# A decode attention kernel on one core: the TensorE program as a four-turn loop of 664 instructions, with one V buffer and column-tiled output projections

## The chip, the cores and the metric

The kernel runs on one core of one Trainium2 chip. The metric is the device time of one execution in microseconds (us). The profile shows one execution of it; its span runs from the first to the last instruction of the program and is shorter than the time (by 1.4 to 1.8 us in nearly all runs here; one exception matters below).

Engines: PE is the matrix engine (TensorE), DVE the vector engine, ACT the scalar engine, POOL GpSimd, SP the engine whose queue issues the loads. Sixteen DMA engines carry the loads (the profile counts 16, and each large load has sixteen landings in the trace).

## The reference, cut to what matters

One decode step: layer norm, a sliding window attention over a cache (window 2048, 16 query heads on 8 KV heads of 256), an output projection, and a gate from a small FFN.

```python
xn = _layernorm(x)                                   # x: (2, 1, 448)
q = xn @ wq                                          # wq: 448 x 4096
k, v = last W = 2048 rows of k_cache, v_cache        # (2, 8, 8192, 256) each
o = softmax(q k^T * 256**-0.5) v
s = o @ wo                                           # wo: 4096 x 448
g = silu(relu(xn @ w1) @ w2)                         # w1: 448 x 1792, w2: 1792 x 448
return x + s * g
```

All is bf16. Nearly all work is loading: 16.8 MB of K, 16.8 MB of V, 10.5 MB of weights. The term s * g is small beside x. So agreement with the reference says little about the attention.

## The kernel before

The attention is cut into four units (one batch element and four KV heads each), with two K and two V buffers. A recording layer collects every engine's operations and emits them in a straight line, with semaphore waits between engines.

```python
def load_k(u):
    d_k[u] = pr.dma(SP, kbuf[u % 2][:, :], kv_src(u, A_k_cache), [st.get(("T", u - 2))])

def load_v(u, cuts=(0, NT)):
    deps = [None if u == 0 else st["q_mm"] if u == 1 else st["PV", u - 2]]
    ...
        d_v[u].append((hi, pr.dma(SP, vbuf[u % 2][:, lo * DH:hi * DH], ..., deps)))
```

T is the transpose of K on DVE, S the scores, Pt the turning of the probabilities, PV the product with V (all PE). The loads stand on the SP queue in the order wq (first part), k0, wq (rest), k1, v0, w1, w2, k2, v1, k3, v2, v3 (two parts), wo. wo comes in seven parts of 9, 7, 5, 4, 3, 2 and 2 row blocks j, and PE works through them at the end:

```python
WO_PARTS = [9, 7, 5, 4, 3, 2, 2]
...
for j in range(2 * NWO):                     # 32 row blocks of wo
    if j == 4:
        attend_spread(3)
    deps = deps + [d_wo.get(j), st["at_z", j // NWO]]
    for i in range(4):                       # four matmuls of 112 columns into one bank of 8 rows
        lo = j * D + i * NCOL
        m_o = pr.op(PE, mm(obk[0:NROW, 0:NCOL], at_z[:, ...], wo_sb[:, lo:lo + NCOL],
                           j == 0 and i == 0, j == 2 * NWO - 1 and i == 3), deps)
# [cut] tmp = obk * g, out = tmp + x, store
```

`idle_work(n)` runs n matmuls whose result nobody reads; they are there to keep PE's clock up.

Of the kernel before, what the change touches and what calls it, by code (L numbers as in the profile page):

```python
# [14 lines left out]
class _Op:  # L15
    __slots__ = ("eng", "fn", "deps", "dma", "needed", "value", "sem")

    def __init__(self, eng, fn, deps, dma):
        self.eng, self.fn, self.deps, self.dma = eng, fn, deps, dma
        self.needed, self.value, self.sem = dma, 0, None  # L20


class _Prog:


    def __init__(self, nc, es):
        self.nc, self.es = nc, es
        self.lists = {PE: [], DVE: [], ACTE: [], SP: [], POOL: []}

    def op(self, eng, fn, deps=()):  # L30
        o = _Op(eng, fn, [d for d in deps if d is not None], False)
        self.lists[eng].append(o)
        return o
# [6 lines left out]
    def run(self):  # L40
        n = 0
        for ops in self.lists.values():
            for o in ops:
                for d in o.deps:
                    d.needed = True
        for e, ops in self.lists.items():
            sem, count = self.es.enter_context(self.nc.semaphore(f"s_{e}")), 0
            for o in ops:
                if o.dma:
                    n += 1  # L50
                    o.sem, o.value = self.es.enter_context(self.nc.semaphore(f"d_{n}")), 16
                elif o.needed:
                    count += 1
                    o.sem, o.value = sem, count

        def emit(eng, ops):
            seen = {}
            for o in ops:
# [4 lines left out]
                for key, (sem, value) in want.items():  # L63
                    if value > seen.get(key, 0):
                        eng.wait_ge(sem, value)
                        seen[key] = value
                made = o.fn(eng) if o.fn else None
                if o.needed:
                    made.then_inc(o.sem, 16 if o.dma else 1)

        for name, e in (("gpsimd", POOL), ("sync", SP), ("scalar", ACTE), ("vector", DVE), ("tensor", PE)):
            emit(getattr(self.nc, name), self.lists[e])


def bass_recurrent_scan__sliding_block_cached__dense_activation_relu__decode_kernel(
# [21 lines left out]
    NU = 4  # L97
# [6 lines left out]
    WO_PARTS = [9, 7, 5, 4, 3, 2, 2]  # L104
    NWO = 16
# [5 lines left out]
    with es:  # L111
# [32 lines left out]
        qz = named("qz", [128, 16 * 64], BF)  # L144
# [15 lines left out]
        q_t = et[:, :].bitcast(F32).tensor  # L160
        ssum = named("ssum", [128, 1], F32)
        rs = named("rs", [128, NU], F32)
        pt = [named(f"pt{i}", [128, 512], BF) for i in range(2)]
# [37 lines left out]
        def load_k(u):  # L201
            d_k[u] = pr.dma(SP, kbuf[u % 2][:, :], kv_src(u, A_k_cache), [st.get(("T", u - 2))])

        def load_v(u, cuts=(0, NT)):
            deps = [None if u == 0 else st["q_mm"] if u == 1 else st["PV", u - 2]]
            d_v[u] = []
            for lo, hi in zip(cuts, cuts[1:]):
                d_v[u].append((hi, pr.dma(SP, vbuf[u % 2][:, lo * DH:hi * DH],
# [14 lines left out]
        p_z = [pr.op(POOL, lambda e, t=t: e.memset(t[:, :], 0.0)) for t in (qrep, spread, h_z, at_z)][-1]  # L223

        a_z = [pr.op(ACTE, lambda e, t=t: e.memzero(t[:, :])) for t in (obk, sbk, hbk, obk_last)][-1]
# [40 lines left out]

        def mm(out_ap, lhsT, rhs, start, stop=False, **kw):
# [15 lines left out]
        def do_T(u, blk):  # L283
            src = kbuf[u % 2][:, :].bitcast(F32).tensor
            dst = kt[blk][:, :].bitcast(F32).tensor
            st["T", u] = st["kt", u, blk] = pr.op(DVE, lambda e: e.transpose(  # L286
# [3 lines left out]
        def do_S(u, blk):  # L290
            b, v = divmod(u, 2)
            deps = [st["q"], st["kt", u, blk], st.get(("exp", u - 1)), a_z]
            for par in range(2):
                for i in range(4):
                    lo = 64 * (4 * i + 2 * v + b) + 8 * (2 * blk + par)
                    o = pr.op(PE, mm(sbk[32 * i:32 * i + 8, :], qz[:, lo:lo + 8], view(kt[blk], 2 * i + par, [[64, NT], [8, 8]]),
                                     blk == 0 and par == 0, blk == NBLK - 1 and par == 1, tile_position=(0, 32 * i)), deps)
                    deps = []
            st["S", u, blk] = o

        def softmax(u, fill=()):
            fill = list(fill)

            def meanwhile():
                if fill:
                    fill.pop(0)()

            meanwhile()
# [6 lines left out]
            meanwhile()  # L315
            a = st["exp", u] = pr.op(ACTE, lambda e: e.activation(  # L316
                e_sb, sbk[:, :], ACT.Exp, bias=bias[:, 0:1], accum_out=ssum[:, 0:1]),
                [v, st.get(("e_t", u - 1)), st.get(("gs", u - 1))])
            v = st["e_t", u] = pr.op(DVE, lambda e: e.transpose(e_t, e_sb), [a, st.get(("Pt", u - 1))])  # L319
            deps = [v, v_sp, st.get(("pt", u - 1))]  # L320
            for x in range(4):
                for g in range(4):
                    lo = 128 * (4 * x + g)
                    o = pr.op(PE, mm(view(pbk, 2 * x, [[8, 16], [1, 2]]), spread[:, lo:lo + 128],
                                     view(et, 512 + 2 * g, [[32, 16], [1, 2]]), g == 0, g == 3), deps)
                    deps = []
            st["Pt", u] = o
            v = st["pt", u] = pr.op(DVE, lambda e: e.tensor_tensor(  # L328
                out=view(pt[u % 2], 0, [[8, NT], [2, 4], [1, 2]]), in0=view(pbk, 0, [[2, NT], [0, 4], [1, 2]]),
                in1=view(hmask, 0, [[0, NT], [1, 4], [0, 2]]), op=ALU.mult), [o, v_hm, st.get(("PV", u - 2))])  # L330
            meanwhile()
            m = st["gs", u] = pr.op(PE, mm(mbk_ap(130, 1), gsum[:, :], ssum[:, 0:1], True, True), [v_gs, a, st["mbk"]])
            st["rs", u] = st["mbk"] = pr.op(DVE, lambda e: e.reciprocal(rs[:, u:u + 1], mbk_ap(130, 1)), [m])
            assert not fill
# [4 lines left out]
        def do_PV(u, gs=range(4)):  # L339
            bank, src, p = out_bank(u), vbuf[u % 2], pt[u % 2]  # L340
            for g in gs:
                deps = [next(d for hi, d in d_v[u] if hi >= 16 * g + 16), st["pt", u], a_z, st["obk"] if u < NU - 1 else None]
                for a in range(2):
                    for i in range(4):
                        t = 16 * g + 4 * i + 2 * a
                        o = pr.op(PE, mm(bank[32 * i:32 * i + 16, :],
                                         p[:, 8 * t:8 * t + 16], src[:, t * DH:(t + 2) * DH],
                                         g == 0 and a == 0, g == 3 and a == 1, tile_position=(0, 32 * i)), deps)
                        deps = []
            st["PV", u] = o  # L350

        def attend_scale(u):
            v = st["osb", u] = pr.op(DVE, lambda e: e.tensor_scalar(  # L353
                out=o_sb[:, :], in0=view(out_bank(u), 0, [[1, 512]]), scalar1=rs[:, u:u + 1], scalar2=None, op0=ALU.mult),
                [st["PV", u], st["rs", u], st.get(("oT", u - 1))])
            if u < NU - 1:
                st["obk"] = v

        def attend_turn(u):
            deps = [st["osb", u], v_fold, st["mbk"]]  # L360
# [6 lines left out]
            st["at", u] = st["mbk"] = pr.op(DVE, lambda e: e.tensor_tensor(  # L367
# [4 lines left out]
        def attend_spread(u):  # L372
            b, v = divmod(u, 2)
            o = st["m_at", u] = pr.op(PE, mm(mbk_ap(256, NWO), at_exp[:, :], fold16[:, :], True, True),
                                      [st["at", u], v_fold16, st["mbk"]])
            st["at_z", v] = st["mbk"] = pr.op(DVE, lambda e: e.tensor_copy(
                view(at_z, NWO * GAP * v + 3 + 4 * b, [[GAP, NWO]]), mbk_ap(256, NWO)), [o, p_z])

        def do_q():
# [8 lines left out]
            v = st["obk"] = pr.op(DVE, lambda e: e.tensor_scalar(  # L388
                out=q_n[:, :], in0=obk[:, :], scalar1=SCALE, scalar2=None, op0=ALU.mult), [o])
            m = pr.op(PE, mm(pbk[:, :], qrep[:, :], q_n[:, :], True, True), [v, v_qr])  # L390
            v = pr.op(DVE, lambda e: e.transpose(view(q_t, 0, [[1, 512]]), view(pbk, 0, [[64, 8], [1, 2], [2, 32]])), [m])
            for r in range(2):
                st["q"] = pr.op(DVE, lambda e, r=r: e.tensor_tensor(
                    out=view(qz, r, [[64, 16], [8, 8], [2, 4]]), in0=view(q_t, 256 * r, [[1, 16], [32, 8], [0, 4]]),
                    in1=view(gmask, 0, [[0, 16], [0, 8], [1, 4]]), op=ALU.mult), [v, v_gm])

        def do_H():
            deps = [st["w1"], v_xr, a_z]
# [11 lines left out]

        def do_F():
            deps = [st["w2"], st["h"]]
            for f in range(14):
                for i in range(4):
                    lo = W2_AT + f * D + i * NCOL
                    o = pr.op(PE, mm(view(fbk, 0, [[1, NCOL]], n=NROW), h_z[:, f * GAP + 3 - i:f * GAP + 3 - i + NROW],
                                     w2_sb[:, lo:lo + NCOL], f == 0 and i == 0, f == 13 and i == 3), deps)
                    deps = []
            st["F"] = o
            f_ap = view(fbk, 0, [[1, NCOL]], n=NROW)  # L420
            a_e = pr.op(ACTE, lambda e: e.activation(ea[:, :], f_ap, ACT.Exp, scale=-1.0), [o])
            st["a_e"] = a_e

        def gate():
            f_ap = view(fbk, 0, [[1, NCOL]], n=NROW)
            v_d = pr.op(DVE, lambda e: e.tensor_scalar(
                out=ea[:, :], in0=ea[:, :], scalar1=1.0, scalar2=None, op0=ALU.add), [st["a_e"]])
            v_rc = pr.op(DVE, lambda e: e.reciprocal(tmp[:, :], ea[:, :]), [v_d])
            st["g"] = pr.op(DVE, lambda e: e.tensor_tensor(
                out=g_sb[:, :], in0=f_ap, in1=tmp[:, :], op=ALU.mult), [v_rc])  # L430

        def idle_work(n):
            deps = [st["q"], p_id]
            for _ in range(n):
                pr.op(PE, mm(wbk[:, :], ident[:, :], q_n[:, :], True, True), deps)
                deps = []

        def scores(u):
            for blk in range(NBLK):
                do_T(u, blk)  # L440
                if u == 1 and blk == 3:
                    do_H()
                if blk == 1 and u > 1:
                    attend_turn(u - 2)
                if blk == 2 and u > 1:
                    attend_spread(u - 2)
                do_S(u, blk)

# [89 lines left out]
```

## Time and profile before

| | before |
|---|---|
| time, median | 111.43 us (111.37 to 111.62, 4 runs) |
| span of the profiled run | 109.8 us |
| loads | 44.11 MB |
| PE program (compiled instructions) | 1234 |
| last landing of a load | 107.33 us |
| last wo matmul ends | 107.93 us |

From the page of the kernel before: the span, the engines' busy time, and the DMA queues with packets, megabytes and the share of all sixteen engines' span that they took.

```profile
span 109.8 us, 1386 instructions
PE 61.3 (56%) x610; PEld 21.9 (20%) x612; DVE 61.7 (56%) x87; ACT 9.6 (9%) x18; POOL 3.1 (3%) x10
...
q1 hardware_dynamic: 3008, 44.11, 94.9%
q8 instruction: 4, 0.07, 0.2%
q10 hardware_dynamic: 36, 0.01, 0.0%
q14 instruction: 1, 0.01, 0.0%
```

No compute engine is busy for much over half of the span. Queue 8 carries four packets of instructions.

The table of stretches of the kernel before; the last three columns are PE's granted clock, the DMA engines' mean busy share and GB/s.

```profile
core 0: us, PE busy (x) PEld busy (x) DVE busy (x) ACT busy (x) POOL busy (x), PEclk, DMA share, GB/s
...
45.00:61.00 16.00, 11.66 (x158) 5.57 (x150) 10.02 (x14) 0.92 (x3) 0.00 (x0) 0.93 1.02 433
61.00:78.00 17.00, 11.00 (x87) 2.28 (x87) 12.53 (x17) 0.78 (x2) 0.00 (x0) 0.70 1.00 432
78.00:100.00 22.00, 16.34 (x138) 4.33 (x140) 13.46 (x17) 0.78 (x2) 0.00 (x0) 0.79 0.99 422
100.00:107.00 7.00, 6.52 (x121) 5.86 (x121) 1.08 (x3) 0.00 (x0) 0.00 (x0) 1.00 0.84 328
```

From 15 to 100 us the DMA share is 0.99 to 1.02. The loads bound the kernel.

The end of the chain that ended last, kernel before (start, length, what):

```profile
76.42 24.57 DMA kbuf<-in_A_wo_dram
...
101.02 0.95 PE obk L268 x16
...
102.09 5.86 PE obk L268 x112
...
107.97 0.27 DVE tmp L502
...
108.27 0.26 DVE out_sb L504
```

This view puts the last 7 us down to PE, because PE is busy with wo nearly without a pause. The records of the single instructions say more: PE's last eight matmuls start at 107.38, less than 0.05 us after the last load has landed at 107.33, after a short wait. PE and the loads arrive together here.

Each large load counts sixteen landings in the semaphore records, read here as one for each of the sixteen DMA engines. From the semaphore records of the trace, the landings of the last wo part, kernel before:

```
eleven engines  105.56 to 106.09
one engine      106.51
four engines    107.12  107.22  107.31  107.33
```

And the instruction packets of queues 8 and 14 in the same trace:

```
q8   46.18 us, 1102 ns, 16384 bytes
q14  57.25 us,  333 ns,  8192 bytes
q8   57.34 us, 1099 ns, 16384 bytes
q8   85.36 us, 1087 ns, 16384 bytes
q8  102.43 us, 1038 ns, 16384 bytes
```

Four packets of 16 KiB, four engines late by about 1.2 us; one packet of 8 KiB, one engine late by 0.5 us. In the same records one of sixteen landings is late after the first packet (w2: 49.83, the others by 48.53), two after the second (K: 59.47 and 59.55, besides the 58.75 of the 8 KiB packet; the others by 58.24), three after the third (95.78 to 96.01, besides 95.15; the others by 94.68). The records do not number the engines; that each packet hit another one is read from these counts.

### The profile page before, as it was taken

To read this page: it belongs to the slowest core of one execution; us is meant where nothing else is said; L and a number is where in the kernel's file an instruction comes from. 1 tells how busy PE (TensorE), PEld (TensorE's weight loads), DVE (VectorE), ACT (ScalarE), POOL (GpSimd) and SP (SyncE) were. 2 spreads that over 40 slices of the span, in tenths; PEclk is the share of its full clock that TensorE was granted. 3 is DMA by queue.
4 is the path that set the end of the run, shared out by engine and by line. 5 is a ranking of instruction groups with operands and counts; after the bars stand their busy time and mean duration, and the time that the engine had idled before them with its cause. 6 is when DMAs were issued, how large, how long until landed. Compare 5 with 4: busy or idle time off the path is not lost.

```text
span 109.8 us, 1386 instructions
## 1 busy us (share of the span) xinstructions
PE 61.3 (56%) x610; PEld 21.9 (20%) x612; DVE 61.7 (56%) x87; ACT 9.6 (9%) x18; POOL 3.1 (3%) x10
## 2 busy tenths in 40 slices
PE   0000000192699035999970498834039885997993
PEld 0000000020110030034930010112001011533992
DVE  1258039987200679986165999257499926504001
ACT  4990000000000200000200000020000002000000
POOL 7400000000000000000000000000000000000000
PEclk9999999999999965699998555799555699999999
DMA  4989989999899889998999999999999999899950
GB/s 69 505 382 418 501 379 403 448 513 394 382 454 501 382 374 416 415 532 382 418 474 430 394 406 513 406 394 418 501 406 394 445 430 430 361 414 412 393 208 1
DMA packets 3049, 44.19 MB, mean 402 GB/s; under 512 B 354, under 2 KB 612, under 8 KB 1508
## 3 DMA queue, kind: packets, MB, share of 16 engines
q1 hardware_dynamic: 3008, 44.11, 94.9%
q8 instruction: 4, 0.07, 0.2%
q10 hardware_dynamic: 36, 0.01, 0.0%
q14 instruction: 1, 0.01, 0.0%
HBM read 44.11 MB, written 0.00 MB: 402 GB/s over the span
## 4 chain that ended last, share of the span: by engine, by line
DMA 67%; DVE 18%; PE 11%; ACT 1%; issue 1%; SPq 0%
DMA kbuf<-in_A_k_cache_dram 45%; DMA kbuf<-in_A_wo_dram 22%; DVE kt L286 14%; PE obk L268 7%; PE sbk L268 4%; ACT et L316 1%; DVE et L319 1%; DVE rm L309 1%; PE pbk L268 1%; PE mbk L268 1%; DVE o_sb L353 1%; SPq L36 0%; DVE at_exp L367 0%; DVE tmp L502 0%; DVE out_sb L504 0%
## 5 line engine op out<-in xcount | busy, mean ns | idle before, releaser
L268 PE MATMUL sbk<-kt,qz 128*8 128x512 bf16 x128 | 31.1, 1072 | 17.4 <-DVE kt L286 15.2
L286 DVE STREAM_TRANSPOSE kt<-kbuf 128x2048 f32<-128x2048 f32 x16 | 35.9, 2286 | 7.4 <-DMA kbuf<-in_A_k_cache_dram 7.4
L268 PE MATMUL obk<-vbuf,xr 128*4 128x512 bf16 x28 | 3.2, 625 | 13.2 <-DMA vbuf<-in_A_wq_dram 13.2
L309 DVE TENSOR_REDUCE rm<-sbk 128x1 f32<-128x512 f32 x4 | 2.8, 692 | 12.3 <-PE sbk L268 12.3
L316 ACT ACTIVATE et<-sbk,bias 128x512 bf16<-128x512 f32 x4 | 2.7, 682 | 65.1 <-DVE bias L313 65.1
L268 PEld LDWEIGHTS sbk<-kt,qz 128*8 128x8 bf16 x128 | 2.2, 87 | 30.7 <-DVE kt L286 23.1
L268 PE MATMUL obk<-kbuf,at_z 128*8 128x112 bf16 x128 | 6.9, 213 | 0.2 <-DMA kbuf<-in_A_wo_dram 0.2
L268 PE MATMUL obk<-vbuf,pt 128*16 128x512 bf16 x96 | 6.4, 381 | 0.0
L268 PEld LDWEIGHTS obk<-kbuf,at_z 128*8 128x8 bf16 x128 | 6.3, 87 | 0.5 <-DMA kbuf<-in_A_wo_dram 0.2
L268 PE MATMUL pbk<-et,spread 128*128 128x32 bf16 x64 | 2.6, 193 | 6.3 <-DVE et L319 6.3
L319 DVE STREAM_TRANSPOSE et<-et 128x512 bf16<-128x512 bf16 x4 | 2.8, 711 | 4.9 <-ACT et L316 4.9
L268 PE MATMUL mbk<-ident,xg 2*128 2x2 bf16 x7 | 0.3, 164 | 8.0 <-DVE xg L235 8.0
L328 DVE TENSOR_TENSOR pt<-pbk,hmask 128x512 bf16<-128x512 f32 x4 | 2.8, 692 | 3.0 <-PE pbk L268 3.0
L268 PEld LDWEIGHTS pbk<-et,spread 128*128 128x128 bf16 x64 | 2.2, 99 | 9.7 <-DVE et L319 9.7
L268 PE MATMUL wbk<-q_n,ident 128*128 128x512 bf16 x14 | 3.7, 379 | 0.3 <-issue 0.3
L268 PEld LDWEIGHTS obk<-vbuf,xr 128*4 128x4 bf16 x28 | 0.8, 114 | 14.7 <-issue 14.7
L502 DVE TENSOR_TENSOR tmp<-obk,g_sb 8x112 f32<-8x112 f32 x1 | 0.3, 261 | 5.6 <-PE obk L268 5.6
L268 PEld LDWEIGHTS obk<-vbuf,pt 128*16 128x16 bf16 x96 | 2.5, 91 | 4.4 <-issue 1.6
L268 PEld LDWEIGHTS fbk<-wf,h_z 128*8 128x8 bf16 x56 | 2.8, 88 | 1.6 <-issue 1.6
L268 PE MATMUL fbk<-wf,h_z 128*8 128x112 bf16 x56 | 2.9, 213 | 0.0
L367 DVE TENSOR_TENSOR at_exp<-mbk,qmask 128x128 bf16<-128x128 f32 x4 | 1.2, 292 | 3.0 <-PE mbk L268 2.9
L268 PE MATMUL obk_last<-vbuf,pt 128*16 128x512 bf16 x32 | 2.3, 380 | 0.0
(69 smaller groups left out, 39.4 us busy)
## 6 DMA issues: line engine op xcount, KB each, us to landing
kbuf<-in_A_k_cache_dram SPq DMA_DIRECT2D x4, 4096.0 KB, 29.4
vbuf<-in_A_v_cache_dram SPq DMA_DIRECT2D x3, 4096.0 KB, 37.8
wf<-in_B_w_dram SPq DMA_DIRECT2D x2, 1568.0 KB, 43.1
vbuf<-in_A_v_cache_dram SPq DMA_DIRECT2D x1, 3072.0 KB, 20.8
vbuf<-in_A_wq_dram SPq DMA_DIRECT2D x1, 2560.0 KB, 19.7
vbuf<-in_A_wq_dram SPq DMA_DIRECT2D x1, 1024.0 KB, 5.0
vbuf<-in_A_v_cache_dram SPq DMA_DIRECT2D x1, 1024.0 KB, 22.7
kbuf<-in_A_wo_dram SPq DMA_DIRECT2D x1, 1008.0 KB, 24.6
```

The lines of the kernel that those rows point to most:

```text
L268: return lambda e: e.matmul(out_ap, lhsT=lhsT, rhs=rhs, start=start, stop=stop, skip_group_check=True, **kw)
L286: st["T", u] = st["kt", u, blk] = pr.op(DVE, lambda e: e.transpose(view(dst, 0, [[1, 32 * NT]]), view(src, 32 * blk, [[DH // 2, NT], [1, 3 ...
L309: v = pr.op(DVE, lambda e: e.tensor_reduce(out=rm[:, :], in_=sbk[:, :], axis=AX.X, op=ALU.max), [st["S", u, NBLK - 1]])
L316: a = st["exp", u] = pr.op(ACTE, lambda e: e.activation(e_sb, sbk[:, :], ACT.Exp, bias=bias[:, 0:1], accum_out=ssum[:, 0:1]), [v, st.get(( ...
L319: v = st["e_t", u] = pr.op(DVE, lambda e: e.transpose(e_t, e_sb), [a, st.get(("Pt", u - 1))])
L328: v = st["pt", u] = pr.op(DVE, lambda e: e.tensor_tensor(out=view(pt[u % 2], 0, [[8, NT], [2, 4], [1, 2]]), in0=view(pbk, 0, [[2, NT], [0, ...
L353: v = st["osb", u] = pr.op(DVE, lambda e: e.tensor_scalar(out=o_sb[:, :], in0=view(out_bank(u), 0, [[1, 512]]), scalar1=rs[:, u:u + 1], sc ...
L367: st["at", u] = st["mbk"] = pr.op(DVE, lambda e: e.tensor_tensor(out=view(at_exp, 0, [[16, 8], [8, 2], [1, 8]]), in0=view(mbk, 136, [[1, 8 ...
L502: v_t = pr.op(DVE, lambda e: e.tensor_tensor(out=tmp[:, :], in0=obk[0:NROW, 0:NCOL], in1=g_sb[:, :], op=ALU.mult), [m_o, st["g"]])
```

## The change

The intent: PE's straight program of 1234 instructions becomes a loop of four turns, one for each unit, so that the instruction packets seen beside the loads, four in the trace of the kernel before, no longer come in mid-run. For the loop's instructions to be the same in every turn, units 0 to 2 share one V buffer, the probability tile becomes one, and waits become tokens that are taken back after use. wo and w2 use four column tiles of the array side by side, with fewer instructions; the four partial sums are then folded with a small f32 matmul. The core of the diff:

```diff
+        nc.br("pe_all", engines=[t.engine])
+        with nc.body("pe_all", valid_engines=[t.engine]):
+            top = nc.cur_bb
+            nc.br("pe_visit", engines=[t.engine])       # the visit: jump ahead, and come back
+            nc.switch_bb("pe_back", parent=top)
+            ahead = t.mark_branch_hint_location()       # hint of the last branch, armed here
+            emit(t, pe[:at], seen)
+            with t.Fori(0, turns) as i:
+                # [cut] the parts of a turn, some under t.If(i == n) or t.If(i > n)
+            nc.br("pe_past", engines=[t.engine])
+            nc.switch_bb("pe_visit", parent=top)
+            t.nop()
+            nc.br("pe_back", engines=[t.engine])
+            nc.switch_bb("pe_past", parent=top)
+            emit(t, pe[at + len(loop):], seen)
+            t.reg_add(again, again, 1)
+            t.br_lt(again, 1, on_true="pe_all", on_false="pe_end").branch_hint(ahead)   # never taken
# [cut]
-            deps = [None if u == 0 else st["q_mm"] if u == 1 else st["PV", u - 2]]
+            deps = [None if u == 0 else st["q_mm"] if u == NU - 1 else st["PV", u - 1]]
-                d_v[u].append((hi, pr.dma(SP, vbuf[u % 2][:, lo * DH:hi * DH],
+                d_v[u].append((hi, pr.dma(SP, vbuf[u // (NU - 1)][:, lo * DH:hi * DH],
# [cut]
+        def tiled(bank, z, k, w, lo, first, last, deps):     # column tile k % 4, 448 columns at once
+            g = k % 4
+            return pr.op(PE, mm(view(bank, 0, [[1, D]], n=2, p0=32 * g), view(z, k * GAP + 3, [[4, 2]]), w[:, lo:lo + D],
+                                k < first, k >= last, tile_position=(0, 32 * g)), deps)
+        def fold_tiles(bank_ap, start, stop, deps):          # sel and sums are f32
+            for i in range(4):
+                o = pr.op(PE, mm(bank_ap, sel[:, 3 - i:3 - i + NROW], sums[:, i * NCOL:i * NCOL + NCOL], ...), deps)
# [cut] wo: row blocks 0 to 20 (TILED) tiled, 21 to 31 as before
+        m_t = do_wo(NWO, TILED)
+        idle_work(2)
+        v_w = pr.op(DVE, lambda e: e.tensor_copy(sums[:, :], view(obk, 0, [[1, D]])), [m_t, m_f])
+        do_wo(TILED, TILED + 4)                              # the fourth part
+        fold_tiles(view(hbk, 0, [[1, NCOL]], n=NROW), False, False, [v_w])
+        m_o = do_wo(TILED + 4, 2 * NWO)                      # the last three parts
```

## The prediction

> **What bounds it now.** The loads. The page gives 44.11 MB read over a span of 109.8 us; the table of stretches shows the 16 DMA engines 99 to 102% busy from 15 to 100 us; DMA has 67% of the chain of waits, while PE and DVE are 56% busy. In the trace's packet list each 32 KiB packet takes 1213 ns throughout, so [...]a late one stays late.
>
> Late ones exist. Queue 8 carries four 16,384-byte instruction packets, at 46.2, 57.3, 85.4 and 102.4 us, 1.1 us each: PE's program, about 1,220 instructions and waits. [...]After the first, one of w2's sixteen landings is 1.3 us after the rest. After all four, the last wo part has eleven landings at 105.6–106.1 us, one at 106.5 (an 8 KiB instruction packet of another queue) and four at 107.1–107.3: each fetch hit another engine. PE waits for 107.33, runs its last eight wo matmuls to 107.95; two DVE operations (0.5 us) and the store end it at 109.8.
>
> **What the change does.**
> 1. [...]mid-run fetches should go. [...]Worth at most 1.2 us: the last landing moves to 106.1–106.5. If the visit's fetch collides with the first wq load (from 1.7 us), one engine starts up to 1.2 us late and most is lost.
> 2. wo gets 21 column-tiled steps, four side by side (estimate from PV's 32 matmuls in 2.3 us: 0.06 us a step against 0.21 for four 112-column matmuls), 11 old ones, two f32 folds. PE's wo work (6.9 us) loses about 3 us, but PE already waited for landings, so directly this gains nothing; it lets PE follow earlier landings. The fold (0.7 us DVE copy; four f32 matmuls, estimated 0.4–0.75 us from the f32 ones of the trace) stands before the last three parts: after the part ahead of it lands, PE needs 0.85 + fold + 1.4 = 2.65–3.0 us, against 2.5 for the DMA limit. PE becomes the limit by 0.2–0.5 us.
> 3. One V buffer: v1 now waits for PV0 (about 53 us; k2 keeps DMA busy to 58), v2 for PV1 (about 72; k3 lasts to 77). Slack 3–5 us: no gap expected.
> 4. Branches, tokens and turn_q per unit (2 x 0.36 us DVE, from 0.725 us for the larger product at most halved): under the loads.
>
> Sum: last landing −1.0, PE tail +0.3: 110.7 us. Some weight lies on a colliding visit (no gain), less on refetches at the back edge. Range 109.9 to 112.2. Faster by over 2% 0.03, within 2% 0.88, slower by over 2% 0.09.
>
> **What would show it.** Step 1: queue 8 is empty after 5 us, and the last wo part's sixteen landings lie within 0.6 us, near 106.1; more packets, or one engine 1 us late from the first load on, refute it. Step 2: PE no longer waits for the last landing and ends at 106.9–107.4. Step 3: DMA over 97% busy from 15 to 100 us; a dip near 58 or 77 refutes it. Step 4: each unit's T starts when its K lands.
>
> **What would make it wrong.** [...]the visit colliding; a fold over 1 us; a late V load.

The sum comes to 110.7 us: 111.4 of before, −1.0 for the last landing and +0.3 for PE's tail. The landings listed above show the lag staying.

## The result, and the profile after

| | before | after |
|---|---|---|
| time, median | 111.43 us | 112.12 us (111.9 to 112.12, 4 runs) |
| ratio of fast runs | | 1.0054 (1.0036 to 1.0071) |
| span of the profiled run | 109.8 us | 110.7 us |
| PE program | 1234 | 664 |
| instruction packets of 16 KiB | 4 | 1, at 3.70 us |
| last landing | 107.33 us | 107.63 us |
| last wo matmul ends | 107.93 us | 108.81 us |

A ratio is the mean time of one kernel's fast runs over that of the other's of the same rounds, so it is not quite the ratio of the medians quoted. The change is slower by 0.5%, clear of noise, though within 2%.

The same lines of the page, kernel after:

```profile
span 110.7 us, 1292 instructions
PE 59.8 (54%) x526; PEld 17.7 (16%) x528; DVE 62.9 (57%) x96; ACT 10.2 (9%) x19; POOL 3.1 (3%) x11
...
q1 hardware_dynamic: 3008, 44.11, 94.2%
q8 instruction: 1, 0.02, 0.1%
q10 hardware_dynamic: 36, 0.01, 0.0%
q14 instruction: 1, 0.01, 0.0%
```

Three of the four packets are gone. The table of stretches, kernel after:

```profile
45.00:61.00 16.00, 11.60 (x120) 3.02 (x116) 11.16 (x17) 0.78 (x2) 0.00 (x0) 0.82 1.02 436
61.00:78.00 17.00, 10.77 (x87) 2.44 (x87) 11.82 (x16) 0.78 (x2) 0.00 (x0) 0.70 1.00 432
78.00:100.00 22.00, 15.86 (x141) 4.83 (x142) 14.27 (x18) 0.78 (x2) 0.00 (x0) 0.86 0.99 422
100.00:107.00 7.00, 5.87 (x59) 2.60 (x59) 2.48 (x7) 0.25 (x1) 0.00 (x0) 1.00 0.81 318
```

The shared V buffer did not starve the loads: up to 100 us the DMA shares are those of before. v1 was issued at 54.05 and v2 at 73.10, as forecast. So the loss does not come from the middle.

The end of the chain, kernel after:

```profile
76.55 29.12 DMA kbuf<-in_A_wo_dram
...
105.71 3.11 PE hbk L350 x52
...
108.84 0.27 DVE tmp L597
...
109.14 0.26 DVE out_sb L599
```

That load ended at 105.67, the landing of the fourth part; from there on PE has 3.11 us of work without a pause. The end of PE's timeline, kernel after (start, busy time, what):

```profile
105.71 0.95 PE L350 MATMUL hbk<-kbuf,at_z 128*8 128x112 bf16 x16
106.50 0.93 PE L350 MATMUL hbk<-sums,sel 128*8 128x112 f32 x8
107.27 1.54 PE L350 MATMUL hbk<-kbuf,at_z 128*8 128x112 bf16 x28
```

By their starts, the sixteen matmuls of part four take 0.79 us, the f32 fold 0.77 (four matmuls, eight in the records), the last 28 matmuls 1.54. PE is now behind the last landing by 1.18 us (108.81 less 107.63), where before it was 0.60.

And the landings (from the semaphore records), kernel after:

```
first wq part (of the start):  fifteen engines 5.11 to 5.66, one 7.11
last wo part:                  fourteen engines 105.62 to 106.17, one 106.64, one 107.63
```

One engine is 1.5 us late from the first load on, and it is still 1.5 us late at the end: in every large load from wq to wo one landing is 1.44 to 1.53 us behind the ones on time (1.45 in the first, 1.46 in the last). The one 16 KiB packet stands at 3.70 us, 926 ns long, when the first loads have been running for 2 us. The packet records, though they do not number the engines, suggest how the lag arises: the load packet that begins as the instruction packet ends, at 4.61, took 812 ns, where others of its size take 313 (median). In the kernel before, too, each of the four 16 KiB packets is followed, within 0.02 us of its end, by a load packet 243 to 479 ns longer than the median of its size. An estimate from these records: the lag is the 0.9 to 1.1 us of the instruction packet and the 0.24 to 0.5 us more of the load packet behind it (926 and 499 ns in the changed kernel, 1.43 us, against 1.45 measured).

In these two executions two differences add: the last landing is 0.30 us later than before, and PE ends 0.58 us further behind it. Together 0.88 us; the spans differ by 0.84, the medians of the time by 0.69. Only the second is shown to come from the change. In the profiled runs below that have a packet during the loads, whether one, two or four, the last landing lies anywhere from 107.29 to 107.63 (leaving out two runs in which a load was cut, and one in which all loads were held back).

### The profile page after: what moved, and what is told of

Same layout as the page of the kernel before. It is cut to its first block, busy times and chain, and to the rows that moved or that the text cites. A ratio compares the mean times of both kernels' runs of the same rounds, so it can differ in the third digit from the quotient of the medians.

```text
span 110.7 us, 1292 instructions
## 1 busy us (share of the span) xinstructions
PE 59.8 (54%) x526; PEld 17.7 (16%) x528; DVE 62.9 (57%) x96; ACT 10.2 (9%) x19; POOL 3.1 (3%) x11
## 5 line engine op out<-in xcount | busy, mean ns | idle before, releaser
L350 PE MATMUL wbk<-q_n,ident 128*128 128x512 bf16 x19 | 4.9, 380 | 1.5 <-DVE qz L385 1.4
L350 PE MATMUL obk<-vbuf,pt 128*16 128x512 bf16 x96 | 5.8, 381 | 0.0
L350 PE MATMUL fbk<-wf,h_z 128*2 128x448 bf16 x14 | 1.7, 566 | 1.7 <-DVE h_z L483 1.7
L350 PE MATMUL hbk<-kbuf,at_z 128*8 128x112 bf16 x44 | 2.5, 213 | 0.0
L350 PE MATMUL obk<-kbuf,at_z 128*2 128x448 bf16 x21 | 2.0, 351 | 0.9 <-DMA kbuf<-in_A_wo_dram 0.7
L350 PEld LDWEIGHTS wbk<-q_n,ident 128*128 128x128 bf16 x21 | 1.7, 97 | 3.9 <-DVE qz L385 1.6
L350 PEld LDWEIGHTS hbk<-kbuf,at_z 128*8 128x8 bf16 x44 | 2.2, 87 | 0.6 <-DMA kbuf<-in_A_wo_dram 0.5
```

The costliest lines, as they stand in the source:

```text
L350: return lambda e: e.matmul(out_ap, lhsT=lhsT, rhs=rhs, start=start, stop=stop, skip_group_check=True, **kw)
```

## The experiments

The theory: (a) every 16 KiB instruction packet makes one DMA engine 1.2 to 1.5 us late for good, whenever it comes, and since different packets hit different engines it makes no difference whether there are one or four; (b) the f32 fold makes PE the limit behind the fourth part. Rivals: the lag has another cause; the visit is worse than a packet in mid-run; the loop refetches at its back edge; the tiling costs something other than the fold.

Groups of runs that went to the chip together share their runs of before, whose medians were 111.33 to 111.50. The groups ran on different chips, so times of two groups are best compared through their ratios to before.

### The fold in bf16 (fold_bf16)

```diff
-        sel = named("sel", [128, GAP], F32)
-        sums = named("sums", [128, D], F32)
+        sel = named("sel", [128, GAP], BF)
+        sums = named("sums", [128, D], BF)
```

> Only the two folds are in bf16 instead of f32, so four single matmuls each instead of eight passes. Theory (the last 3.1 us of PE after the landing at 105.67 are the limit, and the fold is 0.77 us of it): the wo fold takes about 0.25 us, PE then follows the last landing at 107.6 with 0.6 us, so PE ends near 108.3 and the time falls by 0.5 us to 111.6. Rival (the end is set by the late last landing alone, the fold is hidden): no change, 112.1. The landings themselves must not change in either.

Measured: 111.33 us (111.28 to 111.42), ratio to before 0.9972 (0.9914 to 1.0029; one run of before stood out at 112.53, with a span of 110.1 like the rest). The last landing was 107.50, PE ended at 108.10. PE's timeline:

```profile
105.53 0.95 PE L352 MATMUL hbk<-kbuf,at_z 128*8 128x112 bf16 x16
106.32 0.36 PE L352 MATMUL hbk<-sums,sel 128*8 128x112 bf16 x4
106.52 1.58 PE L352 MATMUL hbk<-kbuf,at_z 128*8 128x112 bf16 x28
```

The fold takes 0.20 us from start to start instead of 0.77, and PE is 0.60 us behind the last landing as in the kernel before. Against the changed kernel the median fell by 0.8 us (ratios to before 0.9972 and 1.0054), more than the 0.5 forecast. Part (b) holds.

### The tiling alone, on the kernel before (tile_only, tile_bf16)

The kernel before with straight PE code and two V buffers, but `tiled`, `fold_tiles` and the end of the changed kernel (the second with the bf16 edit above):

```diff
-            for i in range(4):
-                m_o = pr.op(PE, mm(obk[0:NROW, 0:NCOL], at_z[:, ...], wo_sb[:, lo:lo + NCOL], ...), deps)
+        m_t = do_wo(NWO, TILED)
+        # [cut] copy, do_wo(21, 25), fold, do_wo(25, 32), as in the changed kernel
```

> The kernel before, with only wo and w2 tiled and folded as in the changed kernel; no loop, two V buffers, its PE program still streamed. Theory (tiling brings the fold onto the end of the chain): packets and landings as before, last landing about 107.3, but PE runs 3.1 us after the landing at 105.4 and ends at 108.5 instead of 107.9, time 112.0 (0.6 over before). Rival (tiling is harmless or helps, the loop or the V buffer costs): 111.4 or less.

> The kernel before with only wo and w2 tiled, folded in bf16. Theory (the f32 fold behind the fourth wo part is what the tiling costs; with it cheap, PE follows the last landing at 107.3 to 107.5 by 0.6 us as before): PE ends at 107.9 to 108.1, time 111.5, within 0.2 of before and 0.6 under the f32 tiling. Rival (the tiling costs something else, for instance the DVE copy or the split into two banks): it stays at 112.0 or more.

Measured: tile_only 112.13 us (ratio 1.0044, 0.9985 to 1.0102, with the same outlying run of before), tile_bf16 111.43 (1.0012, 0.9995 to 1.0029). tile_only had four 16 KiB packets, the last landing at 107.57, and PE at the end like this:

```profile
105.65 0.95 PE L274 MATMUL hbk<-kbuf,at_z 128*8 128x112 bf16 x16
106.43 0.93 PE L274 MATMUL hbk<-sums,sel 128*8 128x112 f32 x8
107.20 1.54 PE L274 MATMUL hbk<-kbuf,at_z 128*8 128x112 bf16 x28
```

It ended at 108.74, nearly where the changed kernel ended. The interval of its ratio takes in 1, because of that one outlying run; the other six runs of before, 111.31 to 111.59, all lie below its four, 112.00 to 112.19. So tiling with the f32 fold is enough for a loss of the same size; no further cost or gain of the loop and the single V buffer is seen. In bf16 the tiling costs nothing that can be seen and gains nothing (ratio 1.0012), since PE was waiting for landings before.

### Without the visit and the hint (plain_loop), hint alone (hint_only, hint_bf16), visit alone (visit_only)

```diff
-            nc.br("pe_visit", engines=[t.engine])
-            nc.switch_bb("pe_back", parent=top)
-            ahead = t.mark_branch_hint_location()
             emit(t, pe[:at], seen)
             ...
-            t.br_lt(again, 1, on_true="pe_all", on_false="pe_end").branch_hint(ahead)
```

> The changed kernel without the early visit, the hint and the outer loop that carries it; PE runs head, loop, tail. Theory (any instruction packet costs one engine 1.2 to 1.5 us, whenever it comes before the end): no packet at 3.7 us, one or two later ones of 16 KiB between 30 and 100 us, each making one further engine 1.2 to 1.5 us late; last landing 107.2 to 107.7, time 112.0 within 0.4. Rival (the early visit is what hurts, a mid-run packet would be free): last landing near 106.6 and time 111.1. Second rival (the loop's way back needs refetching): four or more packets and a time above 113.

> The changed kernel without the visit, with the branch hint at the head and the outer loop that carries it. The trace of the changed kernel shows that the visit's branches take 0.32 and 0.18 us, no stall[...]. Theory A (the visit causes that packet[...]; the hint keeps the later ones away): no 16 KiB packet at all, the landings of the last wo part within 0.6 us but for the engine of the 8 KiB packet, near 106.1 and 106.6, PE ends at about 107.8, time 111.1. Theory B (the hint causes the packet, 0.3 us before it in the held run): a packet at 3 to 4 us as before, time 112.1. Theory C[...]: one or two packets later, last landing 107.3 to 107.6, time 112.0.

> The same with the folds in bf16. Theory A: no 16 KiB packet, last landing 106.6, PE ends 0.6 us later at 107.2, time 110.5, under before by 0.9. Theory B or C: last landing 107.5 as with the bf16 folds alone, time 111.3.

> The changed kernel with the visit but without the hint. Theory A: the packet at 3.7 us is there, and others may follow[...] near 100 us. Theory B: no packet at 3.7 us, packets at about 33 and 102 us as in the plain loop.

The 16 KiB packets and the last landings, from the trace records:

```
               16 KiB packets at (us)   last landing   PE ends   time (us)
changed kernel 3.70                     107.63         108.81    112.12
visit_only     3.65, 100.52             107.58         108.74    112.07 (one run)
hint_only      32.98                    107.51         108.73    112.25
plain_loop     32.89, 102.21            107.51         108.65    111.98
hint_bf16      32.92                    107.29         107.91    111.29
```

For the hint without the visit, theory C was right and A and B were not. For the visit without the hint, what A said came true: the visit does bring the early packet, and a second one followed near 100 us. Each of these kernels has at least one packet. The first comes at 3.65 or 3.70 us with the visit and at 32.89 to 32.98, in the first turn, without it; what sets it off is not shown, since the records do not name the instructions in it. With the hint there was no further one near 100 us, without it there was one at 100.52 or 102.21. All four f32 kernels have the same time within 0.3 us: early or in mid-run, one packet or two, the last landing is at 107.5 to 107.6. The rival that an early packet is worse fell with it; so did the refetching loop, since no turn after the first made a packet.

Instruction packets are not the only thing that makes engines late. In visit_only and in fold_bf16 about fifteen load packets of 32 KiB between 57 and 60 us took 1.3 to 2.1 us instead of 1.21, with only the 8 KiB packet near, and in visit_only seven of the sixteen last landings are at 106.67 or later, after two 16 KiB packets. The last landing of all, 107.58 and 107.50, was no later than in the others. What slowed these packets is not known.

The visit itself never stalled PE. Its two branches took 0.32 and 0.18 us in the trace of the changed kernel, at 0.91 and 1.29 us, long before the packet at 3.70. So neither of them waited for this packet. Which instructions it holds, and why it came then, is not shown.

### Which DMA engine is late (probe, less_on_11, less_on_15)

Eight tiny loads of n = 8 to 15 rows behind the last wo part:

```diff
+        probes = [pr.dma(SP, scr[0:n, 32 * (n - 8):32 * (n - 7)], A_wo[0:n, 0:32]) for n in range(8, 16)]
```

> The changed kernel plus eight tiny loads of 8 to 15 rows at the very end of the load queue[...]. Theory (one fixed engine lost 1.5 us to the early instruction packet and stays behind): each tiny load lands at about 106 us until it is wide enough to include that engine, and from that width on its last landing is at 107.6; the second step, of 0.5 us, shows the engine of the 8 KiB packet. Rival (the lag is a property of the single load, for instance of the order of its descriptors, not of an engine): no step, all eight land together. Time within 0.4 us of the changed kernel.

Which engines a load runs on no trace shows. The traces show only counts: each tiny load has one immediate semaphore update and n landings for its n rows, and the loads of 121 and 120 rows in the next two runs have 11 and 15. The reading needs more, that a load of n + 1 rows runs on the engines of a load of n rows and on one more; that is not shown. Measured: 112.33 us (one run, its state unknown). The late engine's wo landing was at 107.59. The latest landings of the tiny loads were 106.93, 107.12, 107.31 and 107.49 for n = 8 to 11, all before that, and from n = 12 on a new one appears at 107.77. So, if the assumption holds, the engine that n = 12 adds was late in this run; the author called it number 11. The reading is not clean: the tiny loads queue up behind each other by 0.2 us each, and the engine of the 8 KiB packet could not be made out.

Then the third wo part was cut, at row 121 to leave the late engine less to carry, or as a control at row 120 to leave another one less (on top of fold_bf16; the labels have engine numbers):

```diff
-            d_wo[j0] = pr.dma(SP, wo_sb[:, ...], wo_src[v, :, ...], ...)
+            d_wo[j0] = [pr.dma(SP, wo_sb[p0:p1, ...], wo_src[v, p0:p1, ...], ...)
+                        for p0, p1 in (((0, 121), (121, 128)) if j0 == NWO else ((0, 128),))]   # control: 120
```

> The changed kernel with bf16 folds, and the third wo part (5 row blocks) loaded as rows 0 to 120 and rows 121 to 127[...]. Theory (the late engine is [...]always the same one): its lag of 1.5 us is taken back, the last landing falls from 107.5 to 106.8 to 107.3[...], time 110.8 to 111.1, under the 111.3 of the bf16 folds and under before. Rival (another engine in another run): last landing 107.5 or later, time 111.3 or more.

> Control: the same cut at row 120[...]. Theory: [...]time 111.3 as with the bf16 folds alone. If this gains as much as the cut at row 121, the gain there is not from unloading the late engine.

The control was expected to leave the last landing at 107.5.

Measured: 116.25 us (114.61 to 117.52) and 115.81 (113.41 to 117.82), 2 to 6% slower than before (less_on_11 by its fast runs 1.048). Both failed, and for a reason that neither expectation had: the packets themselves became slow. From the packet records, the mean of the 128 packets of 4480 bytes of that part:

```
changed kernel  179 ns      less_on_11  334 ns      less_on_15  301 ns
```

With that part cut in two, at either row, its packets take 1.7 to 1.9 times as long, and so do those of the next part, which was not cut (the 3584-byte packets rose from 144 to 243 and 247 ns). Why is not shown: the records do not tell which rows an engine carried, and the change of rows and the second load came together. The lag could not be taken back this way, and whether it is always the same engine that is late stays open.

### Loads held back until the visit is over (hold_loads)

```diff
             nc.switch_bb("pe_back", parent=top)
+            t.nop().then_inc(back, 1)
...
+        nc.sync.wait_ge(back, 1)          # ahead of the first load
```

> The changed kernel, but the load queue waits until PE is back from its visit, so that the early instruction packet has the DMA engines to itself. Theory (the packet makes an engine late only because the loads are already running): loads start about 4 us later (5.5 to 6.5 us), the sixteen landings of the first wq part lie within 0.6 us of each other, no engine is 1.5 us late any more, and the distance from the first load packet to the last landing of wo shrinks from 105.9 to about 104.9 us (the engine of the 8 KiB packet is then the last). Time 112.1 + 4 - 1 = about 115. Rival (that engine is slow by itself): it is 1.5 us late again and the distance stays 105.9, time above 116.

Measured: 113.22 us (112.84 to 113.34), ratio 1.0164. The visit was over so early that the first load began at 2.60 us instead of 1.73, not 4 us later. The packet now ran from 1.94 to 2.93, nearly ahead of the loads, and the sixteen landings of the first wq part lay between 5.94 and 6.41: no engine 1.5 us late. So far the theory holds. But the distance from the first load packet to the last landing was 105.8 us, as in the changed kernel (105.9), where 104.9 was expected: between 5.6 and 7.3 us about a dozen packets of the first K load took 1.6 to 2.3 us instead of 1.21, and spread the engines by 1.45 us again. Why, no run here tells; in visit_only and fold_bf16 it happened with nothing held back. As a test of what the packet is worth at the end, this run failed.

### A program with no packet (no_fetch, pad_fetch; no_fetch_warm, pad_fetch_warm; two_blocks, three_blocks)

To have no packet at all, the PE program was made shorter still; that 435 to 457 instructions would be short enough was the author's estimate. These kernels give a wrong result: on top of hint_bf16 they leave out PE work, but make every load in the same order. The control of each pair adds matmuls that are jumped over and never run, which makes the program 133 instructions longer.

```diff
-                do_H()
-                do_F()
+                pass
-            for par in range(2):          # S: half
+            for par in range(1):
-                for a in range(2):        # PV: half
+                for a in range(1):
-        idle_work(10)                     # put back in the second and third pair
# the control of each pair:
+            t.br_lt(again, 1, on_true="pe_skip", on_false="pe_pad")
+            nc.switch_bb("pe_pad", parent=top)
+            for _ in range(65):
+                self.pad(t)               # never executed
+            nc.br("pe_skip", engines=[t.engine])
```

> Wrong result on purpose: the version with the hint, without the visit, with bf16 folds, and with so much PE work left out (the FFN matmuls, half of S and PV, part of the filler) that its PE program has 437 instructions[...]; every load is still made, in the same order. Theory (one late engine per 16 KiB packet is what keeps the end of the loads at 107.3 to 107.6): no 16 KiB packet, all landings of the last wo part at or below 106.2 us but for the engine of the 8 KiB packet (106.6), PE ends at about 107.2, time 110.5. Rival 1[...]: one packet near 33 us and last landing 107.3 to 107.6, time 111.3. Rival 2 (the late engine has another cause): no packet and yet a landing at 107.3 or later.

> Control for the last: the same wrong-on-purpose program with 65 never executed matmuls (130 instructions) in front of its last branch, which is never reached by them[...]. Nothing that runs differs. Theory: one 16 KiB packet near 33 us[...], one engine 1.2 to 1.5 us late from there on, last landing 107.3 to 107.6, time 0.7 to 1.0 us over the unpadded one. If both make a packet, or both none, the times are equal within 0.3.

> Wrong on purpose, as no_fetch, but with the ten filler matmuls ahead of the last PV put back (457 instructions[...]). In no_fetch the landings were as the theory had them (no 16 KiB packet, fifteen landings at most 106.20, one at 106.63), but the granted clock stood at 0.50 from 84 to 105 us and PE ended at 109.0, 2.4 us after the last landing. Theory (only the missing filler made PE late there): the clock is back at 1.0 before 100 us, no 16 KiB packet, last landing 106.6, PE ends at 107.2 to 107.4, time 110.5 to 110.8. If the packet comes back the last landing is at 107.4 and the time 111.3.

> Control: the same with the never executed matmuls[...]. Theory: one 16 KiB packet near 95 us, last landing 107.3 to 107.6, PE ends 0.6 us later, time 0.6 to 1.0 us over no_fetch_warm, at 111.3. Rival: equal times.

> Wrong on purpose, as no_fetch_warm, with a little more PE work cut so that 435 instructions remain with the filler in. In no_fetch_warm the span was as forecast (last landing 106.59, PE end 107.19, span 109.05), but the time lay 4.5 to 5.1 us over the span instead of 1.4 to 1.8: a 16 KiB packet came at 110.5 us, after the last store[...]. Theory: without that packet the time is span plus 1.5, so 110.5 to 110.9; last landing 106.6, PE end 107.2 to 107.6. Rival (the excess at the end has another cause): time above 113 again.

> Its control with the never executed matmuls: one packet near 95 us, last landing 107.3 to 107.6, time 112.0 to 112.4 as pad_fetch_warm, so 1.2 to 1.8 us over two_blocks; of that about 0.9 us is the landing and the rest PE, which waits longer for wo, loses its clock and runs the part behind it slower.

That PE would lose its clock was taken from the control before: in pad_fetch_warm PE waited 1.79 us for wo, and its clock was 0.66 between 100 and 105 us, against 1.00 in no_fetch_warm. It did not part this pair: three_blocks waited 0.97 us and had 0.74, two_blocks waited 0.73 us and had 0.67.

The instruction queues on the page of no_fetch, and then of its control pad_fetch:

```profile
q1 hardware_dynamic: 3008, 44.11, 93.8%
q10 hardware_dynamic: 36, 0.01, 0.1%
q14 instruction: 1, 0.01, 0.0%
```

```profile
q1 hardware_dynamic: 3008, 44.11, 93.5%
q8 instruction: 1, 0.02, 0.1%
q10 hardware_dynamic: 36, 0.01, 0.0%
q14 instruction: 1, 0.01, 0.0%
```

What was measured (instructions compiled; packets and landings from the trace records of the profiled run):

```
                instr.  16 KiB packets at  last landing  PE ends  span    time (us), all runs
no_fetch        437     none               106.63        109.03   110.9   111.77 to 112.35
pad_fetch       570     96.83              107.42        109.54   111.4   112.04 to 113.26
no_fetch_warm   457     110.49             106.59        107.19   109.1   113.64 to 115.17
pad_fetch_warm  590     96.95              107.52        108.72   110.6   112.17 to 112.53
two_blocks      435     none               106.74        107.89   109.7   110.92 to 111.49
three_blocks    568     95.58, 110.03      107.39        109.02   110.9   111.21 to 113.03
```

With 435 and 437 PE instructions no 16 KiB packet was seen, with 457 one after the last store, with 568 to 664 at least one during the loads, and with 1234 four. The landings are settled. Without a 16 KiB packet during the loads the last landing is at 106.59 to 106.74 in three kernels of three, and fourteen or fifteen of the sixteen are at 106.20 or earlier; the one or two behind them are 0.4 to 0.6 us late, as after the 8 KiB packet, which is there in all. With a packet it is at 107.39 to 107.52 in three of three, though not one executed instruction of the loop or of the end differs, apart from one branch. Part (a) of the theory holds for the landing: the packet makes the last engine late, by 0.65 to 0.93 us in these three pairs. (The packet of pad_fetch came at 96.83 and not near 33 us as expected; the later expectations were set by this.)

Its worth in time is not settled, since PE spoilt it three times, each in its own way. In no_fetch the filler matmuls were gone and PE ran at half clock (0.50 from 84 to 105 us). Stretches of no_fetch, and then of no_fetch_warm, where the ten filler matmuls are back (the third number from the right is the granted clock):

```profile
95.00:100.00 5.00, 3.13 (x29) 1.10 (x29) 1.56 (x4) 0.25 (x1) 0.00 (x0) 0.50 1.01 422
100.00:105.00 5.00, 4.57 (x23) 0.95 (x24) 1.39 (x4) 0.00 (x0) 0.00 (x0) 0.50 1.01 397
```

```profile
95.00:100.00 5.00, 4.26 (x33) 1.30 (x32) 1.27 (x3) 0.25 (x1) 0.00 (x0) 0.69 1.00 418
100.00:105.00 5.00, 4.76 (x44) 1.52 (x45) 2.31 (x6) 0.00 (x0) 0.00 (x0) 1.00 1.02 400
```

(The filler does not fix the clock by itself: one execution of no_fetch, of 111.77 us, had a mean clock of 0.95 over its span where the other three had 0.69.) With the clock back, no_fetch_warm's span was exactly the forecast: last landing 106.59, PE 0.60 us behind it, span 109.05, the shortest of all profiled runs. But its time was 4.5 to 5.1 us over its span instead of 1.4 to 1.8. A 16 KiB packet came at 110.49, after the last store and after the end of the span. no_fetch_warm has 20 instructions more than no_fetch; why the packet came so late is not shown. two_blocks, two instructions shorter than no_fetch, has no such packet, and its time is 1.4 to 1.8 us over the span again; packet and excess went together. (three_blocks also has a late packet, but at 110.03, before its store went out at 110.43, and its time is only 1.4 to 1.7 us over its span.) The time of two_blocks missed the forecast all the same (111.27, not 110.5 to 110.9): PE's clock fell back to 0.67 between 100 and 105 us, and PE ended 1.15 us behind the last landing. And three_blocks scattered from 111.21 to 113.03, so that the two ratios to before (0.9982 and 0.9983, of fast runs alone) show no difference in time. The record also has the span of every execution, which leaves out what follows the last store. By the means of the fast runs it is 110.4 against 111.3, 109.6 against 110.75, and 109.6 against 110.2 us, always shorter without the packet, by 0.6 to 1.2 us. Only in the middle pair do the single spans not overlap (109.1 to 110.3 against 110.6 to 110.8), and there PE has a part in it: in the profiled runs it ended 0.60 and 1.20 us behind the last landing. How much of the landing's 0.65 to 0.93 us reaches the time with a full PE program could not be tried: the full program has 664 instructions, and none of 568 or more ran here without a packet during the loads.

### A smaller last part (last_small)

On hint_bf16:

```diff
-    WO_PARTS = [9, 7, 5, 4, 3, 2, 2]
+    WO_PARTS = [9, 7, 5, 4, 3, 2, 1, 1]
```

> A version that should do a little better: hint without visit, folds in bf16, and the last wo part of two row blocks split into two parts of one, so that four matmuls instead of eight are left after the last landing. Theory: same landings (last 107.3), PE ends 0.4 instead of 0.6 us after it, time 111.1 against 111.4 of before. Rival (the extra part costs the queue as much): 111.3 or more.

Measured: 111.37 us, ratio 0.9976 (0.9917 to 1.0035). No gain is shown. PE ended 0.62 us behind the last landing at 107.50, because it did not have to wait for it: from the fourth part's landing at 105.55 it had 2.53 us of work without a pause. No run here beats the kernel before clear of noise; the bf16 versions (111.29 to 111.43) tie with it.

## Why the prediction was wrong

- **Sum: 110.7 us predicted, 112.12 measured.** The predicted gain of 0.7 us became a loss of 0.7.
- **Step 1, "Worth at most 1.2 us: the last landing moves to 106.1–106.5", counted as −1.0: failed.** It is the term that turned the sign. The packets in mid-run did go, as said. But the landing went from 107.33 to 107.63. The prediction named the colliding visit and gave it a small weight. It should have been the main case: the same text noted that lags do not add because each fetch hits another engine. From that it follows that removing three of four packets is worth nothing, and that only a program with no packet at all can bring the gain. Nothing in the trace said that the one remaining packet would come before the first load, where it might have been harmless; it came at 3.70 us, 2 us into the loads. The runs without any packet show what the step can bring: a last landing at 106.6 to 106.7, a gain of 0.6 to 0.7 and not 1.0, presumably because the engine of the 8 KiB packet is then the last or near it (the last one or two landings are 0.4 to 0.6 us late there). Only the programs of 435 and 437 instructions ran here without a 16 KiB packet.
- **Step 1, the visit: right in effect.** With it the packet came early, at 3.70 us, and none followed. Its two branches, 0.32 and 0.18 us, were over before that packet began.
- **Step 2, "PE becomes the limit by 0.2–0.5 us": right in kind, slightly short.** It was 0.58 us. The three terms behind the fourth part measured 0.79 + 0.77 + 1.54 = 3.1 us, against 0.85, a fold of 0.4 to 0.75, and 1.4. tile_only shows that this step alone brings 0.6 to 0.7 us in the medians. It would have spoilt the forecast even if step 1 had come true. An estimate from the changed kernel's own landings: without its one late engine the fourth part would have landed at 104.66 instead of 105.67, and PE's 3.1 us of work behind it would have ended near 107.8, only 0.1 to 0.2 us ahead of the 107.93 of before.
- **Step 3, the V buffer: right.** v1 was issued at 54.05 (forecast 53), v2 at 73.10 (forecast 72), and the DMA shares show no dip.
- **Step 4, branches, tokens and the turning of q: right.** From the visit on, the branches of the changed kernel take 0.07 to 0.32 us in the trace records, and PE's last 3.11 us of work, without a pause, wait for none.
- **Refetches at the back edge did not occur**; no turn after the first made a packet in any variant (in the tables above the packets of the loop kernels came at 3.65 to 3.70, near 33, and from 95.58 us on).

## What to carry to other kernels

In these kernels an engine that fell behind stayed behind (1.45 us in the first load, 1.46 in the last), and the latest one set the end of the loads; so look at the sixteen landings of the last load, not at mean shares: one packet with 0.1% of the DMA time moved the last landing by 0.65 to 0.93 us in the three pairs. Taking away three of four packets brought nothing (last landing 107.33 before, 107.63 after), and only with none left during the loads did it fall (106.59 to 106.74); so count what remains after a change, not what goes. And put a fold or any other PE work that needs no late data ahead of the last landings, or make it cheap: 0.77 us of f32 fold behind the fourth of seven parts was the whole visible loss here, and in bf16 it took 0.20.
